# Pooled attention and a GELU layer on one core: v over 128 partitions, first batch two head pairs at a time

## The chip, the cores and the metric

The kernel runs on one core of a Trainium2 chip. The metric is the device time of an execution in microseconds (us), lower is better. The engines of the core work side by side and wait for each other on semaphores: TensorE (PE; its weight loads are listed apart as PEld), VectorE (DVE), ScalarE (ACT), GpSimd (POOL) and SyncE (SP). SP, ACT and POOL also start DMAs.

## What is computed

A batch has 8 heads, 576 rows and 64 columns a head; there are 8 batches. k and v are averaged over every 8 rows, which leaves 72 rows a head; each row of q attends to them. The result, 4608 rows of 512, goes through two matrix products with a tanh GELU between them.

```python
k_p = k.reshape(B, H, Sp, 8, D).mean(axis=3)          # v_p alike; Sp = 72
scores = scale * q @ k_p.transpose(0, 1, 3, 2)
attn = exp(scores - max); attn = attn / attn.sum(-1)
x = (attn @ v_p).transpose(0, 2, 1, 3).reshape(4608, 512)
h = x @ w_in                                          # 512 x 2048
out = gelu_tanh(h) @ w_out                            # 2048 x 512
```

## The kernel before

**Two kinds of work on one TensorE.** The attention runs by batch, 576 rows each; the two products run by group, 512 rows each, nine groups. Batch 0 is done first, alone. Then, in group g, the first product (`p1_mm`, L282: 16 tiles `fo` of 128 columns, each a sum over four slices `ko`) is followed by the second product (`p2_mm`, L291: four row tiles r, each a sum over 16 `fo`), and the attention of batch g+1 is put between the matmuls of the second product, at the positions `pos` of its 64 matmuls. Groups 7 and 8 have no attention.

**Attention of a batch.** k is loaded into 128 partitions: a main part of four rows each and a tail of 64 rows (L70, L71). v is loaded with the pooled row as partition (L79), so 72 partitions, 8 heads each. VectorE makes the pools by three additions each (L145, `k_steps`, `v_steps`). TensorE transposes pooled k (L172) and, for batches 0 and 1, q (L189); later q are transposed by a DMA that SP starts (L200). A pair of heads `pr` and a half of the rows `c` (288 of the 576) make one step of eight: scores (`qk`, L211), exponential (`expo`, L218), product with v (`av`, L231, in batch 0 L236), and the division by the sum: logarithm (L244, L245; in batch 0 L247), exponential of its negative (L249), and a multiplication on VectorE into `xT` (L257). The sums come from columns of eights that stand beside v's (in batch 0 from a tile `ones`).

**PSUM** has eight banks. Tile `fo` of a group goes to the bank that `h_bank` names, the second product's row tile to `o_bank`; VectorE copies it to `osb` (L296) and stores follow on SP (L302). The fourth tile (`fo` = 3) of a group uses the bank of the last row tile of the group before.

**The order is the program's.** There is no scheduler: each engine runs its instructions in the order in which the program issues them, and so does each DMA queue. What VectorE does beside the first product stands in `plan`: after which tile `fo` which step of the next batch comes. The products on a tile of zeros (`spin`, L312), called fillers here, put nothing to use.

**DMA order.** At the start SP loads half of k and all of v, ACT half of k and k's tail; POOL loads q, two quarters of w_in, then k and q of batch 1, two more quarters and w_out in four parts (4 MB in memory for each weight, cast to bf16 on the way). In group g, POOL loads q of batch g+2, SP transposes it by DMA, and POOL waits for that (`gate`, L358) before it loads k and v.

Of the kernel before, what the change touches and what calls it, by code (L numbers as in the profile page):

```python
# [18 lines left out]
def kernel(  # L19
# [29 lines left out]
    kvp = ctx.enter_context(tc.tile_pool(name="kvp", bufs=2))  # L49
# [12 lines left out]
    vs, qs = {}, {}  # L62
    kts = [consts.tile([128, KR + 1, 512], F32, name=f"kt{i}") for i in range(2)]

    def load_k(b, engs):
        rows = k[b].rearrange("h (j l) d -> (h j) (l d)", l=8)
        main = rows[0:128 * KR].rearrange("(p r) c -> p r c", r=KR)
        n = KR // len(engs)
        for i, eng in enumerate(engs):
            eng.dma_start(out=kts[b % 2][:, i * n:(i + 1) * n], in_=main[:, i * n:(i + 1) * n])  # L70
        engs[-1].dma_start(out=kts[b % 2][64:128, KR], in_=rows[128 * KR:])  # L71

    def load_v(b, eng, h0=0, h1=H):
        if b not in vs:
            vs[b] = kvp.tile([Sp, H, 512], F32, name="vt")
        rows = v[b, h0:h1].rearrange("h (j l) d -> j h (l d)", l=8)

        for j0, j1 in ((0, 64), (64, Sp)) if eng is nc.sync else ((0, Sp),):
            eng.dma_start(out=vs[b][j0:j1, h0:h1], in_=rows[j0:j1])  # L79
# [8 lines left out]
    w_in_b = consts.tile([128, KO, DF], BF16, name="w_in_b")  # L88
    w_out_b = consts.tile([128, FO, DM], BF16, name="w_out_b")
    w_in_v = moe_w_in.rearrange("(ko p) f -> p ko f", p=128)  # L90
    w_out_v = moe_w_out.rearrange("(fo p) d -> p fo d", p=128)
# [4 lines left out]
    load_v(0, nc.sync, 0, 4)  # L96
    load_v(0, nc.sync, 4, 8)
# [4 lines left out]
    def load_w_in(i):  # L102
        nc.gpsimd.dma_start(out=w_in_b[:, :, i * 512:(i + 1) * 512], in_=w_in_v[:, :, i * 512:(i + 1) * 512])  # L103

    load_w_in(0)
    load_w_in(1)
# [4 lines left out]
    kTs = [consts.tile([128, 2, H, Sp], BF16, name=f"kT{i}") for i in range(2)]  # L111
    kps = [consts.tile([128, KR + 2, D], BF16, name=f"kp{i}") for i in range(2)]

    vps = [consts.tile([Sp, PR, 2, 2, D], BF16, name=f"vp{i}") for i in range(2)]

    vz = consts.tile([Sp, PR, 2, 2, D], BF16, name="vz")
    ones = consts.tile([Sp, 2, 2, D], BF16, name="ones")
# [5 lines left out]
    nc.vector.memset(kTs[0], 0.0)  # L123
    nc.vector.memset(vz, 0.0)
    nc.vector.memset(ones, 0.0)
    nc.vector.memset(ones[:, 0, 0], 8.0)
    nc.vector.memset(ones[:, 1, 1], 8.0)
    nc.gpsimd.memset(kTs[1], 0.0)  # L128
    nc.gpsimd.memset(kps[1], 0.0)  # L129
    nc.gpsimd.memset(kts[1][0:64, KR], 0.0)  # L130
    nc.gpsimd.memset(vps[0], 8.0)  # L131
    nc.gpsimd.memset(vps[1], 8.0)  # L132

    load_k(1, [nc.gpsimd])
    load_q(1)
    load_w_in(2)
    load_w_in(3)
    for i in range(4):
        nc.gpsimd.dma_start(out=w_out_b[:, 4 * i:4 * i + 4, :], in_=w_out_v[:, 4 * i:4 * i + 4, :])

# [13 lines left out]
    def v_steps(b, hf):  # L154
        t = vs[b][:, hf * 4:(hf + 1) * 4]

        def s3():
            w = (vps[b % 2] if b else vz)[:, 2 * hf:2 * hf + 2]
            for e in range(2):
                add(w[:, :, e, e, :], t[:, e::2, 0:64], t[:, e::2, 64:128])  # L160

        return [lambda: add(t[:, :, 0:256], t[:, :, 0:256], t[:, :, 256:512]),
                lambda: add(t[:, :, 0:128], t[:, :, 0:128], t[:, :, 128:256]), s3]
# [4 lines left out]
    def trans_k(b, bank, odd_eng=None):  # L168
        tp = half_bank(bank)[:, 0:(KR + 1) * 128].rearrange("p (r c) -> p r c", c=128)
        kf = kps[b % 2].rearrange("p r d -> p (r d)")  # L170
        for r in range(KR + 1):
            nc.tensor.transpose(out=tp[:, r, :], in_=kf[:, r * D:r * D + 128], identity=identb)  # L172
        tp = tp[0:D]
        n7 = (H - 1) * KH
        for e in range(2):
            copy = nc.scalar.copy if e and odd_eng is nc.scalar else nc.vector.tensor_copy
            o = kTs[b % 2][e * 64:(e + 1) * 64, e]
            copy(out=o[:, 0:H - 1].rearrange("p h (j r) -> p h j r", r=KR),  # L178
                 in_=tp[:, 0:KR, 0:n7].rearrange("p r (h j) -> p h j r", j=KH))
            copy(out=o[:, H - 1, 0:(128 - n7) * KR].rearrange("p (j r) -> p j r", r=KR),  # L180
                 in_=tp[:, 0:KR, n7:128].rearrange("p r j -> p j r"))
            copy(out=o[:, H - 1, (128 - n7) * KR:], in_=tp[:, KR, 64:128])

    def trans_q(b, i, t0, n, bank, eng):
        if b not in qTs:
            qTs[b] = bp.tile([128, 2, TP, 128], BF16, name="qT")
        tp = half_bank(bank)[:, 0:n * 128].rearrange("p (t c) -> p t c", c=128)
        for x in range(n):
            nc.tensor.transpose(out=half_bank(bank)[:, x * 128:(x + 1) * 128],  # L189
                                in_=qs[b][:, i, (t0 + x) * 128:(t0 + x + 1) * 128],  # L190
                                identity=identb)
        o = qTs[b][:, i, t0:t0 + n]
        if eng is nc.scalar:
            nc.scalar.copy(out=o, in_=tp)
        else:
            nc.vector.tensor_copy(out=o, in_=tp)

# [9 lines left out]

    def qk(b, c, pr, bank):
        for e in range(2):
            h = 2 * pr + e  # L210
            nc.tensor.matmul(out=PS[:Sp, bank + e, :CH].rearrange("j (t p) -> j t p", p=32),  # L211
                             lhsT=kTs[b % 2][:, c, h, :],
# [3 lines left out]
    def expo(b, c, pr, bank):  # L216
        e = ep.tile([Sp, 2, CH], BF16, name="e", bufs=8)
        nc.scalar.activation(out=e, in_=PS[:Sp, bank:bank + 2, :CH], func=ACT.Exp, scale=1.0 / 64.0)  # L218
        es[b, c, pr] = e

    def flat(w):
        return w.rearrange("j a d -> j (a d)")

    def av(b, c, pr, bank):
# [3 lines left out]
        e = es.pop((b, c, pr))  # L228
        for x in range(2):
            if b:  # L230
                nc.tensor.matmul(out=PS[:, bank + x, :CH], lhsT=flat(vps[b % 2][:, pr, x]),  # L231
                                 rhs=e[:, x, :], start=True, stop=True)
            else:
                for y in range(2):
                    w = vz[:, pr, y] if x else ones[:, y]
                    nc.tensor.matmul(out=PS[:, bank + 1 - x, :CH], lhsT=flat(w), rhs=e[:, y, :],  # L236
# [4 lines left out]
    def norm(b, c, pr, bank):  # L241
        ld = ep.tile([128, CH], F32, name="ld")
        if b:
            nc.scalar.activation(out=ld[0:64], in_=PS[64:128, bank, :CH], func=ACT.Ln)  # L244
            nc.scalar.activation(out=ld[64:128], in_=PS[0:64, bank + 1, :CH], func=ACT.Ln)  # L245
        else:
            nc.scalar.activation(out=ld, in_=PS[:, bank + 1, :CH], func=ACT.Ln)  # L247
# [4 lines left out]
    def mult(b, c, pr, bank):  # L252
        rc = rcs.pop((b, c, pr))
        col = b * S + c * CH
        for x in range(2 if b else 1):
            rows = slice(x * 64, (x + 1) * 64) if b else slice(0, 128)
            nc.vector.tensor_tensor(out=xT[rows, pr, col:col + CH], in0=PS[rows, bank + x, :CH],  # L257
                                    in1=rc[rows], op=ALU.mult)

# [9 lines left out]
    def h_bank(g, fo):  # L269
        x, y = x_bank(g), 1 - x_bank(g)  # L270
        if fo == 4:
            return 7
# [7 lines left out]
    def p1_mm(g, fo, ko, c0=0, c1=GROUP):  # L280
        r0 = g * GROUP
        nc.tensor.matmul(out=PS[:, h_bank(g, fo), c0:c1], lhsT=w_in_b[:, ko, fo * 128:(fo + 1) * 128],  # L282
# [22 lines left out]
    act_set(EXP_SET)  # L305
    for s in k_steps(0):
        s()

    def spin(n):

        for _ in range(n):
            nc.tensor.matmul(out=PS[:, 7, :], lhsT=idle[:, 0:128], rhs=idle, start=True, stop=True)  # L312

    def scores(b, c, pr, bank):
        qk(b, c, pr, bank)
        expo(b, c, pr, bank)

    spin(16)
    trans_q(0, *QG[0], 5, nc.scalar)
    trans_q(0, *QG[1], 6, nc.scalar)  # L320
    spin(4)
    trans_k(0, 4, nc.scalar)
    trans_q(0, *QG[2], 5, nc.vector)
    trans_q(0, *QG[3], 6, nc.vector)
    spin(2)
    for i, (c, pr) in enumerate(((0, 0), (0, 1), (1, 0), (1, 1), (0, 2), (0, 3), (1, 2), (1, 3))):
        if i:
            spin(1)
        scores(0, c, pr, (2, 0)[i % 2])
    for hf in range(2):  # L330
        for s in v_steps(0, hf):
            s()

    early = [(fo, ko) for ko in range(KO) for fo in range(4)]
    take = (0, 0, 0, 0, 0, 4, 6, 6)
    for i, (c, pr) in enumerate(ORDER):
        bank = (4, 6, 0, 2, 4, 6, 4, 6)[i]
        av(0, c, pr, bank)
        norm(0, c, pr, bank)
        mult(0, c, pr, bank)  # L340
        if i == 3:

            vs[1] = kvp.tile([Sp, H, 512], F32, name="vt")
            nc.vector.memset(vs[1][:, 0, 0:1], 0.0)
            load_v(1, nc.sync)
        for fo, ko in early[:take[i]]:
            p1_mm(0, fo, ko, 0, CH)
        early = early[take[i]:]


    for g in range(NG):
        nb = g + 1 if g + 1 < B else None
        act_set(GELU_SET)
        if g + 2 < B:
# [5 lines left out]
            load_v(g + 2, nc.gpsimd)  # L360
# [3 lines left out]
        if nb is not None:  # L364
            kk = k_steps(nb)
            v0, v1 = v_steps(nb, 0), v_steps(nb, 1)
            tk = [lambda: trans_k(nb, 4)]
            if g:
                plan = {2: kk[:1], 3: kk[1:], 7: v0[:1], 8: v0[1:], 9: tk, 11: v1[:1], 12: v1[1:]}
            else:  # L370
                tq = [lambda a=a, i=i: trans_q(nb, *a, 4 + i, nc.vector) for i, a in enumerate(QG)]
                plan = {0: kk, 4: tk, 6: tq[:1], 7: tq[1:2], 8: tq[2:3], 9: tq[3:], 10: v0, 12: v1}
# [5 lines left out]
        if g == 0:  # L378
            first = [(fo, ko, CH) for ko in range(KO) for fo in range(4)]
        else:  # L380
            late = 3
            rest = [fo for fo in range(4) if fo != late]
            first = [(fo, ko, 0) for ko in range(2) for fo in rest]
            first += [(late, 0, 0), (late, 1, 0)]
            first += [(fo, ko, 0) for ko in (2, 3) for fo in rest + [late]]
        for fo, ko, c0 in first:
            p1_mm(g, fo, ko, c0)
        for fo in range(FO):
# [4 lines left out]
            for s in side[fo]:  # L393
                s()

# [6 lines left out]
        if nb is not None:  # L402
            act_set(EXP_SET)
            pos = (6, 14, 20, 27, 34, 41, 48, 55, 61)
            for i in range(len(ORDER) + 1):
# [7 lines left out]
                if i:  # L413
                    at(pos[i], norm, *a)
                    at(min(pos[i] + 9, 65), mult, *a)
# [43 lines left out]
```

The softmax here doesn't subtract the row's maximum and nothing guards it: scores larger than these inputs give would overflow.

## Time and profile before

| | |
|---|---|
| median of 8 runs | 311.26 us (310.81 to 312.35) |
| profiled execution | 311.07 us |
| its span | 309.3 us |
| granted clock | 0.998 |
| TensorE, weight loads | 297.6, 149.4 us busy |
| ScalarE, VectorE, GpSimd | 220.8, 157.1, 30.8 us busy |
| group 1, group 4 (start to next start) | 32.12, 31.85 us |
| first product of group 0 from its fifth tile | 25.85 us after the span's start |
| HBM read, written | 36.70, 9.44 MB |

The span is what the profiler sees of the execution, from its first instruction to its last; 1.8 us of the profiled execution lie around it. A product's row says how long it is in the pipeline; the next one starts earlier.

### The profile page before, as it was taken

Reading aid. Unit: us, or ns where it says so; the run is one execution under the profiler, and the core shown is the slowest. Engines: PE = TensorE matmul, PEld = TensorE weight load, DVE = VectorE, ACT = ScalarE, POOL = GpSimd, SP = SyncE. Lnnn points to the kernel's source line nnn. Section 1 sums busy time; section 2 is a strip of 40 time slices with the busy share of each in tenths; the row PEclk is TensorE's granted clock in tenths of the full one; section 3 lists DMA queues with packets and bytes.
Section 4 is the critical chain, followed back from the end, with each engine's and each line's share of the span. In section 5 each row is a group of like instructions: output and inputs, shape, how many; then the busy total and the mean of one; then the engine's idle time right before and its main releaser. Section 6 shows DMA issues by size and latency. Waiting matters only on the chain.

```text
span 309.3 us, 4278 instructions
## 1 busy us (share of the span) xinstructions
PE 297.6 (96%) x1545; PEld 149.4 (48%) x1545; DVE 157.1 (51%) x304; ACT 220.8 (71%) x414; POOL 30.8 (10%) x54
## 2 busy tenths in 40 slices
PE   6788999999999999999999999999999999999994
PEld 2455455445544455445544554455445544444441
DVE  3867536557568356855495459636772640120011
ACT  1597588877987799778987898689868986306500
POOL 8530000301201100120003000200000000000000
PEclk9999999999999999999999999999999999999999
DMA  7999996984985982598258727572101220121022
GB/s 219 238 283 247 180 202 122 271 219 80 279 214 106 245 189 52 110 242 175 69 110 240 175 70 105 168 177 67 40 0 36 51 51 2 34 68 34 2 68 69
DMA packets 32701, 41.05 MB, mean 133 GB/s; under 512 B 17608, under 2 KB 21704, under 8 KB 31784
## 3 DMA queue, kind: packets, MB, share of 16 engines
q0 software_dynamic: 10160, 24.26, 35.5%
q1 hardware_dynamic: 22200, 15.74, 21.7%
q10 hardware_dynamic: 320, 0.79, 0.9%
q8 instruction: 12, 0.20, 0.2%
q14 instruction: 9, 0.07, 0.1%
HBM read 36.70 MB, written 9.44 MB: 149 GB/s over the span
## 4 chain that ended last, share of the span: by engine, by line
PE 84%; DMA 12%; POOL 2%; issue 0%; DVE 0%; POOLq 0%
PE PS L291 39%; PE PS L282 36%; DMA w_out_b<-in_moe_w_out_dram 8%; DMA kt<-in_k_dram 4%; PE PS L231 4%; PE PS L211 4%; PE PS L172 1%; POOL w_in_b L103 0%; POOL kT L128 0%; POOL qb L84 0%; POOL vp L131 0%; POOL vp L132 0%; DVE osb L296 0%; POOL kt L130 0%; POOL kp L129 0%
## 5 line engine op out<-in xcount | busy, mean ns | idle before, releaser
L291 PE MATMUL PS<-w_out_b,gT 128*128 128x512 bf16 x576 | 136.4, 379 | 0.2 <-DMA w_out_b<-in_moe_w_out_dram 0.2
L282 PE MATMUL PS<-xT,w_in_b 128*128 128x512 bf16 (+2 forms) x592 | 129.0, 373 | 0.6 <-DMA w_in_b<-in_moe_w_in_dram 0.3
L288 ACT ACTIVATE gT<-PS 128x512 bf16<-128x512 f32 x144 | 81.2, 603 | 47.6 <-PE PS L282 47.4
L282 PEld LDWEIGHTS <-w_in_b 128*128 128x128 bf16 x592 | 57.3, 98 | 65.5 <-issue 2.0
L291 PEld LDWEIGHTS <-gT 128*128 128x128 bf16 x576 | 56.0, 97 | 57.2 <-issue 1.0
L296 DVE COPY osb<-PS 128x512 f32<-128x512 f32 x36 | 24.9, 691 | 95.4 <-PE PS L291 95.3
L257 DVE TENSOR_TENSOR xT<-PS,rc 64x288 bf16<-64x288 f32 (+1 forms) x120 | 54.5, 455 | 29.0 <-ACT rc L249 26.7
L218 ACT ACTIVATE e<-PS 72x576 bf16<-72x576 f32 x64 | 40.6, 643 | 8.6 <-PE PS L211 7.7
L145 DVE TENSOR_TENSOR vt<-vt 72x1024 f32<-72x1024 f32 (+1 forms) x32 | 30.5, 953 | 6.8 <-DMA vt<-in_v_dram 6.1
L249 ACT ACTIVATE rc<-ld 128x288 f32<-128x288 f32 x64 | 28.3, 442 | 2.0
L211 PE MATMUL PS<-qT,kT 128*72 128x288 bf16 x128 | 26.1, 286 | 0.1
L244 ACT ACTIVATE ld<-PS 64x288 f32<-64x288 f32 x56 | 22.8, 407 | 1.3
L245 ACT ACTIVATE ld<-PS 64x288 f32<-64x288 f32 x56 | 22.5, 402 | 1.3
L263 ACT ACT_TABLE_LOAD x17 | 21.8, 1283 | 2.1 <-issue 1.8
L231 PE MATMUL PS<-e,vp 72*128 72x288 bf16 x112 | 23.1, 285 | 0.0
L211 PEld LDWEIGHTS <-kT 128*72 128x72 bf16 x128 | 14.4, 113 | 14.2 <-issue 1.4
L145 DVE TENSOR_TENSOR kt<-kt 128x1280 f32<-128x1280 f32 (+1 forms) x16 | 18.5, 1158 | 5.2 <-DMA kt<-in_k_dram 4.7
L358 POOL COPY gate<-qT 1x2 bf16<-1x2 bf16 x6 | 1.0, 174 | 154.9 <-DMA qT<-qb 154.9
L178 DVE COPY kT<-PS 64x504 bf16<-64x504 bf16 x15 | 10.1, 675 | 7.2 <-PE PS L172 7.1
L231 PEld LDWEIGHTS <-vp 72*128 72x128 bf16 x112 | 11.0, 98 | 3.3
L312 PE MATMUL PS<-idle 128*128 128x512 bf16 x29 | 9.3, 436 | 1.2 <-DVE idle L120 1.2
L145 DVE TENSOR_TENSOR vp<-vt 72x128 bf16<-72x128 f32 x28 | 6.9, 284 | 0.6
(45 smaller groups left out, 75.3 us busy)
## 6 DMA issues: line engine op xcount, KB each, us to landing
out_dram<-osb SPq DMA_DIRECT2D x142, 64.0 KB, 1.7
kt<-in_k_dram POOLq DMA_DIRECT2D x7, 1024.0 KB, 5.9
vt<-in_v_dram POOLq DMA_DIRECT2D x6, 1152.0 KB, 12.7
qb<-in_q_dram POOLq DMA_DIRECT2D x7, 576.0 KB, 15.4
w_in_b<-in_moe_w_in_dram POOLq DMA_DIRECT2D x4, 512.0 KB, 17.4
w_out_b<-in_moe_w_out_dram POOLq DMA_DIRECT2D x4, 512.0 KB, 24.2
vt<-in_v_dram SPq DMA_DIRECT2D x2, 512.0 KB, 11.3
vt<-in_v_dram SPq DMA_DIRECT2D x1, 1024.0 KB, 11.5
```

What stands on the lines that cost most here:

```text
L145: nc.vector.tensor_tensor(out=o, in0=a, in1=b, op=ALU.add)
L211: nc.tensor.matmul(out=PS[:Sp, bank + e, :CH].rearrange("j (t p) -> j t p", p=32), lhsT=kTs[b % 2][:, c, h, :], rhs=qTs[b][:, h // 4, :, h ...
L218: nc.scalar.activation(out=e, in_=PS[:Sp, bank:bank + 2, :CH], func=ACT.Exp, scale=1.0 / 64.0)
L231: nc.tensor.matmul(out=PS[:, bank + x, :CH], lhsT=flat(vps[b % 2][:, pr, x]), rhs=e[:, x, :], start=True, stop=True)
L244: nc.scalar.activation(out=ld[0:64], in_=PS[64:128, bank, :CH], func=ACT.Ln)
L245: nc.scalar.activation(out=ld[64:128], in_=PS[0:64, bank + 1, :CH], func=ACT.Ln)
L249: nc.scalar.activation(out=rc, in_=ld, func=ACT.Exp, scale=-1.0)
L257: nc.vector.tensor_tensor(out=xT[rows, pr, col:col + CH], in0=PS[rows, bank + x, :CH], in1=rc[rows], op=ALU.mult)
L282: nc.tensor.matmul(out=PS[:, h_bank(g, fo), c0:c1], lhsT=w_in_b[:, ko, fo * 128:(fo + 1) * 128], rhs=xT[:, ko, r0 + c0:r0 + c1], start=(ko ...
L288: nc.scalar.activation(out=gTs[g][:, fo, :], in_=PS[:, h_bank(g, fo), :], func=ACT.Gelu_apprx_tanh)
L291: nc.tensor.matmul(out=PS[:, o_bank(g, r), :], lhsT=gTs[g][:, fo, r * 128:(r + 1) * 128], rhs=w_out_b[:, fo, :], start=(fo == 0), stop=(fo ...
L296: nc.vector.tensor_copy(out=osb, in_=PS[:, o_bank(g, r), :])
```

## The change

It has three parts and some that go with them.

- v is laid out like k: heads 0 to 3 in partitions 0 to 63, heads 4 to 7 in 64 to 127, four heads each, and the last 8 of the 72 pooled rows of all heads in a fifth column `t[:, 4]` (64 partitions). Loads are four DMAs for one or two. The last rows are pooled apart into `vl`, and two DMAs on SP put them beside the others, so that heads 0 to 3 have 72 rows and heads 4 to 7 have 128, of which 56 are zero. kT follows that order, which takes six copies for three; scores, exponential and product with v take 128 rows for heads 4 to 7.
- In batch 0, after the scores, two head pairs go together: products of both, then one logarithm, one exponential and one multiplication of 2 x 288 columns (`norm0`). The first product of group 0 is no longer split by columns; its first four tiles stand in banks 4 to 7. Fillers stand in other places and numbers (22, then one in each of six score steps, then 5, 2 and 3).
- From group 1 on, the fourth tile's first three slices come after three slices of the others; the multiplication of the step before the last comes before the last copy of outputs (62 for 64).
- w_in is loaded in two parts for four, w_out with four of its rows in one piece; the hidden columns are permuted accordingly, so that a tile's weights are every fourth column. On POOL, the second part of w_in comes before q of batch 1, and the fills of tiles after both. In group 0, q, k and v of batch 2 are asked for after the first product, and VectorE's steps come at other tiles.

```diff
-        engs[-1].dma_start(out=kts[b % 2][64:128, KR], in_=rows[128 * KR:])
+        engs[0].dma_start(out=kts[b % 2][64:128, KR], in_=rows[128 * KR:])
+    def load_v(b, engs):
+        rows = v[b].rearrange("h (j l) d -> j h (l d)", l=8)
+        t = vts[b % 2]
+        for i in range(2):
+            engs[-1].dma_start(out=t[32 * i:32 * i + 32, 4], in_=rows[64:, 4 * i:4 * i + 4])
+        for i in range(2):
+            engs[i % len(engs)].dma_start(out=t[64 * i:64 * i + 64, 0:4], in_=rows[0:64, 4 * i:4 * i + 4])
...
-    w_out_v = moe_w_out.rearrange("(fo p) d -> p fo d", p=128)
+    w_out_v = moe_w_out.rearrange("(q p j) d -> p q (j d)", p=128, j=4)
-    load_v(0, nc.sync, 0, 4)
-    load_v(0, nc.sync, 4, 8)
+    load_v(0, [nc.sync, nc.scalar])
+        nc.gpsimd.dma_start(out=w_in_b[i], in_=w_in_v[:, :, i * 1024:(i + 1) * 1024])
...
+    def v_steps(b):
+        t = vts[b % 2]
+        w = (vps[b % 2] if b else vz)[:, :, 0]
+        vl = vls[b % 2]
+        def pools(c):
+            add(t[:, c, 0:256], t[:, c, 0:256], t[:, c, 256:512])
+            add(t[:, c, 0:128], t[:, c, 0:128], t[:, c, 128:256])
+        def last():
+            add(vl, t[0:64, 4, 0:64], t[0:64, 4, 64:128])
+            for i in range(2):
+                nc.sync.dma_start(out=w[64 - 64 * i:72 - 64 * i, 4 * i:4 * i + 4], in_=vl[32 * i:32 * i + 32])
+        def main():
+            for i in range(2):
+                p = slice(64 * i, 64 * i + 64)
+                add(w[p, 4 * i:4 * i + 4], t[p, 0:4, 0:64], t[p, 0:4, 64:128])
+        return pools, last, main
...
+    def norm0(c, pr, bank):
+        ld = ep.tile([128, 2, CH], F32, name="ld0", bufs=1)
+        nc.scalar.activation(out=ld, in_=PS[:, bank + 1:bank + 4:2, :CH], func=ACT.Ln)
+        rc = ep.tile([128, 2, CH], F32, name="rc0")
+        nc.scalar.activation(out=rc, in_=ld, func=ACT.Exp, scale=-1.0)
+        nc.vector.tensor_tensor(out=xT[:, pr:pr + 2, c * CH:(c + 1) * CH], in0=PS[:, bank:bank + 3:2, :CH],
+                                in1=rc, op=ALU.mult)
-        if fo == 4:
+        if g == 0 and fo < 4:
+            return 4 + fo
+        if g and fo == 4:
             return 7
-        nc.tensor.matmul(out=PS[:, h_bank(g, fo), c0:c1], lhsT=w_in_b[:, ko, fo * 128:(fo + 1) * 128],
+        q, j = divmod(fo % 8, 4)
+        nc.tensor.matmul(out=PS[:, h_bank(g, fo), c0:c1], lhsT=w_in_b[fo // 8][:, ko, q * 512 + j:(q + 1) * 512:4],
...
-    for s in k_steps(0):
+    spin(22, 1)
+    t = kts[0]
+    for r in (slice(0, KR), slice(KR, KR + 1)):
+        add(t[:, r, 0:256], t[:, r, 0:256], t[:, r, 256:512])
+    for s in k_steps(0)[1:]:
         s()
+    load_k(1, [nc.gpsimd])
+    load_w_in(1)
+    load_q(1)
...
+    pools, last, main = v_steps(0)
+    pools(slice(4, 5))
+    last()
+    trans_k_mm(0, 4)
+    trans_k_copy(0, 0, 4, upper=False)
+    trans_k_copy(0, 1, 4, upper=False)
     trans_q(0, *QG[0], 5, nc.scalar)
     trans_q(0, *QG[1], 6, nc.scalar)
-    spin(4)
-    trans_k(0, 4, nc.scalar)
+    scores(0, 0, 2)
+    scores(0, 1, 0)
+    trans_k_copy(0, 0, 4, lower=False)
+    trans_k_copy(0, 1, 4, lower=False)
     trans_q(0, *QG[2], 5, nc.vector)
     trans_q(0, *QG[3], 6, nc.vector)
+    for i, (c, pr) in enumerate(((1, 0), (1, 1), (0, 2), (0, 3), (1, 2), (1, 3))):
+        spin(1, 7)
+        scores(c, pr, (2, 0)[i % 2])
+    pools(slice(0, 4))
+    main()
+    def av0(c, pr, bank):
+        for x in range(2):
+            av(0, c, pr + x, bank + 2 * x)
+    early = [(fo, ko) for ko in range(2) for fo in range(4)]
+    av0(0, 0, 4)
+    norm0(0, 0, 4)
+    av0(1, 0, 0)
+    norm0(1, 0, 0)
+    spin(5, 5)
+    av0(0, 2, 4)
+    norm0(0, 2, 4)
+    nc.vector.memset(vts[1][:, 0, 0:1], 0.0)
+    load_v(1, [nc.sync])
+    spin(2, 1)
+    av0(1, 2, 0)
+    norm0(1, 2, 0)
+    spin(3, 5)
+    for fo, ko in early:
+        p1_mm(0, fo, ko)
...
-                plan = {2: kk[:1], 3: kk[1:], 7: v0[:1], 8: v0[1:], 9: tk, 11: v1[:1], 12: v1[1:]}
+                plan = {2: kk[:1], 3: kk[1:], 7: [lambda: pools(slice(0, 5))], 8: [last, main], 9: tk}
-                plan = {0: kk, 4: tk, 6: tq[:1], 7: tq[1:2], 8: tq[2:3], 9: tq[3:], 10: v0, 12: v1}
+                plan = {0: kk, 6: tk, 10: tq[:1], 11: tq[1:2], 12: tq[2:3],
+                        13: tq[3:] + [lambda: pools(slice(0, 5)), last, main]}
-            first = [(fo, ko, 0) for ko in range(2) for fo in rest]
-            first += [(late, 0, 0), (late, 1, 0)]
-            first += [(fo, ko, 0) for ko in (2, 3) for fo in rest + [late]]
+            first = [(fo, ko) for ko in range(3) for fo in rest]
+            first += [(late, ko) for ko in range(3)]
+            first += [(fo, 3) for fo in rest + [late]]
+        if g == 0:
+            load_next()
-                    at(min(pos[i] + 9, 65), mult, *a)
+                    at(min(pos[i] + 9, 62 if i < len(ORDER) else 65), mult, *a)
```

## The prediction

> **What bounds the kernel now.** I read the page's busy times first, then a table of stretches cut at the groups' starts, then the order of time at those seams where a stretch is longer than its work.
>
> ```profile
> span 309.3 us, 4278 instructions
> PE 297.6 (96%) x1545; PEld 149.4 (48%) x1545; DVE 157.1 (51%) x304; ACT 220.8 (71%) x414; POOL 30.8 (10%) x54
> ```
>
> TensorE is the bound, 96% of the span. The stretches (us, length, then busy time of each engine) say where it isn't: the first 25.85 us belong to batch 0, the next 31.82 to group 0, the next ones to groups 1 to 6.
>
> ```profile
> 0.00:25.85 25.85, 19.91 (x132) 12.28 (x133) 15.92 (x34) 15.22 (x32) 14.02 (x25) 1.00 1.05 243
> 25.85:57.67 31.82, 30.33 (x169) 15.40 (x168) 17.55 (x36) 24.38 (x47) 2.93 (x5) 1.00 1.05 188
> 57.67:89.79 32.12, 32.11 (x166) 16.13 (x165) 19.35 (x37) 26.61 (x51) 2.92 (x5) 1.00 0.81 213
> 154.03:185.88 31.85, 31.85 (x166) 16.14 (x165) 19.25 (x37) 26.59 (x51) 2.90 (x5) 1.00 0.61 145
> ```
>
> A clean group takes 31.85 us; groups 1 to 3 take 32.12. Every product of 512 columns starts 0.216 us after the one before it (64 in 13.81 us in the chain), though its row says 379 ns; so behind each printed wait of TensorE 0.16 us more are lost. Groups 7 and 8 run without a gap. What can move is the first 58 us and 0.27 us in each of three groups. In order of time, TensorE, ScalarE and VectorE (start, length, idle before):
>
> ```profile
> 7.30 2.35 DVE L145 TENSOR_TENSOR kt<-kt 128x1280 f32<-128x1280 f32 x2 [3.87 <-DMA kt<-in_k_dram]
> 13.10 1.18 ACT L218 ACTIVATE e<-PS 72x576 bf16<-72x576 f32 x2 [0.51 <-PE PS L211]
> 17.60 0.40 ACT L247 ACTIVATE ld<-PS 128x288 f32<-128x288 f32 x1
> 24.45 0.46 DVE L257 TENSOR_TENSOR xT<-PS,rc 128x288 bf16<-128x288 f32 x1 [0.85 <-ACT rc L249]
> 27.84 0.44 PE L172 MATMUL PS<-identb,kp 128*128 128x128 bf16 x5 [0.96 <-DVE kp L145]
> 35.84 3.63 PE L282 MATMUL PS<-xT,w_in_b 128*128 128x512 bf16 x16 [0.28 <-DMA w_in_b<-in_moe_w_in_dram]
> 46.07 0.81 PE L291 MATMUL PS<-w_out_b,gT 128*128 128x512 bf16 x3 [0.17 <-DMA w_out_b<-in_moe_w_out_dram]
> 57.67 4.53 PE L282 MATMUL PS<-xT,w_in_b 128*128 128x512 bf16 x19
> ```
>
> Batch 0 is a chain: load of k, adds, exponentials from 13.10, first logarithm at 17.60, last multiplication at 24.91; ScalarE has no rest in it. 26 products from 23.58 (six of 288 columns, 16 of 224, four of 512) put the fifth tile of group 0 at 25.85. Group 0 then loses 1.12 us to the adds of k, 0.44 to w_in, 0.33 to w_out, and 0.23 where 0.07 is left before the first transpose of q: 2.12.
>
> [...] The trace has no strided load[...]. [...] Here the first fillers start 0.43 us apart and from 4.1 us on 0.216. [...] the stores here land 1.7 us after issue.
>
> **The change, part by part.**
>
> *Start.* The first add of k no longer waits for k's tail: SP's half is issued at 0.75 and lands 5.8 later, so VectorE starts at 6.6, not 7.30. Adds of 1.22 (as 72x1024), 0.42 (its slope), 0.83 and 0.49 end at 9.7 (before: 10.18). v's last pools and half of kT's copies go behind them: 0.42 + 0.29 + 0.22 and two of 0.45, to 11.6. TensorE transposes k at 9.9 and q, now behind k in its queue, from 10.25; ScalarE's two copies of q begin 0.5 later and take 1.18, to 11.9; the scores take 0.06 and the first exponential follows 0.44 later, at 12.4 (before: 13.10). Eight took 4.6; I add 0.1 for the second half of q, now ahead of the third: ScalarE is free at 17.1. Meanwhile VectorE makes ten small copies of kT (1.4), two of q (0.91), and v's adds of 1.22 + 0.69 + 0.42, ready at 16.3; v has landed, on two queues, before 14 (16.6 before, on one). Eight products of v take 0.98 from 16.3, and the first logarithm starts 0.33 after the last of them started: 17.5, against 17.60.
>
> *Two pairs at a time.* The program's order shows what each filler waits for: the five for the first multiplication, the two for the second, the three for the third. So they lie in the chain. For 576 columns I take 0.65 (logarithm, near the exponential of scores, 0.643), 0.69 (0.442 + 0.25) and 0.755 (0.455 + 288 at 1.04 ns); with hand-overs 2.15 from logarithm to end of multiplication. From 17.5: first multiplication ends 19.65; five fillers 1.08; eight products 0.98; third logarithm at 21.98, 4.48 after the first; third multiplication ends at 24.13; three fillers 0.65 to 24.84; 16 products of 512 columns 3.45: the fifth tile starts at 28.3. The fourth multiplication ends at 25.5, under them. ScalarE does less (4 x 1.34 against 8 x 0.78), but no pair waits for ScalarE alone now. Against 25.85: **+2.45**.
>
> *Group 0.* k of batch 1 is added from 25.5 to 28.3, hidden under the tiles, as its transposes come two tiles later, at 31: 1.12 gone. w_in as two loads of 4 KB rows and w_out in 8 KB rows move the same bytes in half and a quarter of the pieces; w_in was just 0.28 late and is needed 2.5 us later; w_out's first quarter by 40. I take both waits, and that of q (its transposes come at fo 10), as gone: **-2.12**. If the larger rows bring nothing, w_out still lands as before, under a product that starts 0.7 later: at most 0.3 back. What is late next is v's last pools. Their DMA waits on SP for VectorE, whose adds of v follow the fourth copy of q: p1 ends at 28.3 + 11.66 = 39.96 (before: 13.45 less 1.79 of waits), that copy at 39.1, adds 1.49 + 0.83 + 0.22, so issue at 41.7 and landing, 1.7 as for a store, at 43.4. The products of v come 3.27 into the second product, at 43.2: **+0.2** (0.1 to 1.0 for landings of 1.6 to 2.5). Behind them in TensorE's queue stands all else.
>
> *Groups 1 to 3.* Tile 3 waited for the copy of the last outputs (57.87 to 58.56) and xT's third slice for the multiplication behind it. Now the slice's multiplication stands before the copy, its factor ready at 57.41: slice at 58.4 for a use at 58.97, copy done 59.1 for a use at 59.61, fourth slice at 60.0 for 60.26. **3 x -0.27 = -0.81**.
>
> *Hidden in every group.* Twelve kT copies for six add some 0.8 us to VectorE, v's adds over 128 partitions take off 1.6 (4.9 to 3.3): VectorE is busy 19 of 32. v comes in four loads for one, 1.8 us more issue on an idle GpSimd. The two small DMAs stand on SP behind the transposing DMA of q: in group 1 that started at 71.2, 13.5 us in; behind it they'd land at 75.6 for a use at 75.1, 0.5 late. q waits behind w_out, k and v, which end sooner, so I take nothing. Weight loads overlap products of 0.216: 98 ns could double unseen.
>
> Sum: 2.45 - 2.12 + 0.2 - 0.81 = **-0.28**, span 309.0. The profiled execution took 311.07 with a span of 309.3, the median is 311.26: I predict 311.0.
>
> **Rivals.**
> *Fillers are free.* If TensorE's fillers and waits cover time that ScalarE needs anyway, the start stays at 25.85 and the sum is -2.73: 308.5; with half of it, 309.8. For it: ScalarE's work in this stretch shrinks by 0.9. Against: each filler's wait.
> *Half clock (slower).* Between the end of the fillers (22: some 7.4) and the first scores (12.0) stand only 14 transposes, 0.8 us in 4.6; before, 9 in the 3.35 between two runs of fillers, and the clock held. If it falls, a filler and two scores take 0.92 a round, above ScalarE's 0.575: 0.35 in each of some four rounds, 1.4 in all, 312.4. [...]
> *Small DMAs late.* 1 us in group 0 and 0.5 in group 1 more: 312.5.
> *Strided weight loads show.* They count from 216 ns; at 250, 576 x 0.034 = 20 us: 331. Doubled, nothing.
>
> **How the numbers follow.** A measurement of this kernel tells 0.2%, 0.6 us, from no change. The sum as worked, 310.4 to 311.7, has a chance of 0.46 (0.13 of it faster, 0.27 same, 0.06 slower). Free fillers, in whole or in half: 0.26, faster. Half clock 0.16, late DMAs 0.08, strided loads 0.02: slower, 0.26. The last 0.02 are same. Faster 0.39, same 0.29, slower 0.32. The range leaves out the lower half of free fillers and strided loads: 308.8 to 312.7.
>
> **What would show it.** First exponential near 12.4, first logarithm near 17.5, fifth tile of group 0 near 28.3; fillers waiting for the multiplications; no wait of TensorE for k, w_in, w_out in group 0 and one of some 0.2 for v's small DMA; groups 1 to 3 at 31.85; weight loads under 216 ns. Wrong it would be by a fifth tile before 27 or after 29.5, by products 0.43 us apart after 10 us, or by a waiting of SP that reaches the products of v.

## The result, and the profile after

The changed kernel takes 314.01 us (median) against 311.40: a ratio of 1.0086, 95% interval 1.0073 to 1.0100. The forecast was 311.0, at most 312.7. The profiled execution took 312.47 with a span of 310.7, which is 1.4 more than before; it was the only one of twelve whose granted clock was 1.0. The eleven others had 0.988 to 0.995 and took 313.5 to 315.9. So there are two losses to find: 1.4 us that this profile shows, and some 1.5 that it doesn't.

The head of the page, and the stretches cut at the groups' starts (first batch 0, then group 0, group 1, group 4; length, then busy time of TensorE, its weight loads, VectorE, ScalarE, GpSimd):

```profile
span 310.7 us, 4365 instructions
...
PE 299.2 (96%) x1538; PEld 157.1 (51%) x1538; DVE 150.4 (48%) x333; ACT 219.6 (71%) x403; POOL 41.0 (13%) x76
```

```profile
0.00:28.28 28.28, 22.96 (x126) 12.18 (x126) 18.75 (x44) 14.23 (x21) 15.24 (x29) 1.00 1.01 253
28.28:59.96 31.68, 29.79 (x168) 16.05 (x167) 15.01 (x38) 24.02 (x47) 4.41 (x8) 1.00 0.85 207
59.96:91.81 31.85, 31.85 (x167) 17.01 (x166) 18.15 (x41) 26.63 (x51) 4.42 (x8) 1.00 0.86 187
155.51:187.36 31.85, 31.85 (x167) 17.01 (x166) 18.14 (x41) 26.63 (x51) 4.41 (x8) 1.00 0.60 145
```

The start is 2.43 us longer (28.28 for 25.85) and groups 1 to 3 are clean at 31.85, both as forecast. Group 0 should have shrunk by about 1.9 and shrank by 0.14. The order of time shows where it lost that:

```profile
11.66 1.85 ACT L248 ACTIVATE e<-PS 72x576 bf16<-72x576 f32 x3 [0.49 <-PE PS L240]
17.46 0.65 ACT L294 ACTIVATE ld<-PS 128x576 f32<-128x576 f32 x1 [0.98 <-PE PS L269]
19.67 1.24 PE L351 MATMUL PS<-idle 128*128 128x512 bf16 x5 [1.26 <-DVE xT L297]
24.83 5.34 PE L325 MATMUL PS<-xT,w_in_b 128*128 128x512 bf16 x24
30.87 0.44 PE L175 MATMUL PS<-identb,kp 128*128 128x128 bf16 x5
40.87 2.35 DVE L137 TENSOR_TENSOR vt<-vt 128x1280 f32<-128x1280 f32 x2 [1.98 <-DMA vt<-in_v_dram]
43.53 1.56 SPq L159 DMA_DIRECT2D vp<-vl  x2
45.48 0.41 PE L264 MATMUL PS<-e,vp 72*128 72x288 bf16 x2 [1.88 <-DMA vp<-vl]
```

No wait for k, w_in or w_out is left. Instead TensorE stands 2.04 us (1.88 printed and the 0.16 that every such wait hides) for v's small DMA, where 0.2 was forecast. VectorE waited for v until 40.87, and the DMA issued at 43.53 let TensorE go at 45.48; by the semaphore events of the trace it landed at 45.3, 1.8 us after its issue. The account closes: 2.43 - 2.18 (group 0's waits of before, by e10 below) + 2.04 - 0.81 = 1.48, for 1.4 measured.

### The profile page after: what moved, and what is told of

The parts are those of the page before. It is cut to its first block, busy times and chain, and to the rows that moved or that the text cites. A ratio compares the mean times of both kernels' runs of the same rounds, so it can differ in the third digit from the quotient of the medians.

```text
span 310.7 us, 4365 instructions
## 1 busy us (share of the span) xinstructions
PE 299.2 (96%) x1538; PEld 157.1 (51%) x1538; DVE 150.4 (48%) x333; ACT 219.6 (71%) x403; POOL 41.0 (13%) x76
## 4 chain that ended last, share of the span: by engine, by line
PE 85%; DMA 9%; DVE 2%; ACT 1%; ACTq 1%; issue 1%; SPq 0%; DVEq 0%
PE PS L334 39%; PE PS L325 36%; DMA vt<-in_v_dram 9%; PE PS L264 5%; PE PS L240 4%; DVE vt L137 1%; ACTq L79 1%; PE PS L269 1%; DMA vp<-vl 1%; PE PS L175 1%; ACT rc L296 0%; ACT ld L294 0%; PE PS L351 0%; DVE xT L297 0%; DVE osb L339 0%
## 5 line engine op out<-in xcount | busy, mean ns | idle before, releaser
L325 PE MATMUL PS<-xT,w_in_b 128*128 128x512 bf16 x576 | 127.6, 379 | 0.0
L288 DVE TENSOR_TENSOR xT<-PS,rc 64x288 bf16<-64x288 f32 x112 | 51.0, 455 | 32.6 <-ACT rc L280 30.3
L248 ACT ACTIVATE e<-PS 72x576 bf16<-72x576 f32 (+1 forms) x64 | 40.9, 646 | 8.7 <-PE PS L240 7.8
L240 PE MATMUL PS<-qT,kT 128*72 128x288 bf16 (+1 forms) x128 | 26.0, 286 | 1.3 <-ACT qT L215 1.0
L264 PE MATMUL PS<-e,vp 72*128 72x288 bf16 (+1 forms) x112 | 23.1, 286 | 1.9 <-DMA vp<-vl 1.9
L240 PEld LDWEIGHTS <-kT 128*72 128x72 bf16 (+1 forms) x128 | 13.4, 105 | 15.5 <-DVE kT L185 1.0
L137 DVE TENSOR_TENSOR vt<-vt 128x1280 f32<-128x1280 f32 (+5 forms) x18 | 18.8, 1044 | 3.1 <-DMA vt<-in_v_dram 2.8
L137 DVE TENSOR_TENSOR kt<-kt 128x640 f32<-128x640 f32 (+3 forms) x17 | 18.7, 1099 | 1.9 <-DMA kt<-in_k_dram 1.4
L185 DVE COPY kT<-PS 64x288 bf16<-64x288 bf16 (+2 forms) x48 | 13.0, 319 | 6.3 <-PE PS L175 6.1
L264 PEld LDWEIGHTS <-vp 72*128 72x128 bf16 (+1 forms) x112 | 10.9, 98 | 5.9 <-issue 2.1
```

The costliest lines, as they stand in the source:

```text
L137: nc.vector.tensor_tensor(out=o, in0=a, in1=b, op=ALU.add)
L240: nc.tensor.matmul(out=PS[:n, bank + e, :CH].rearrange("j (t p) -> j t p", p=32), lhsT=kTs[b % 2][c][:, h, :n], rhs=qTs[b][:, h // 4, :, h ...
L248: nc.scalar.activation(out=e[:n], in_=PS[:n, bank:bank + 2, :CH], func=ACT.Exp, scale=1.0 / 64.0)
L264: nc.tensor.matmul(out=PS[:, bank + x, :CH], lhsT=window(vps[b % 2][:n], 2 * pr + x), rhs=e[:n, x, :], start=True, stop=True)
```

## The experiments

Theories for the 1.4 us: *late load* (v of batch 1, let go behind the third multiplication at 24.1, lands at 40.7, and all behind it is late), or *backlog* (the DMA engines are full until about 45, and a small DMA lands when what they hold has landed, whenever it is issued). For the 1.5 us that the profile doesn't show: *half clock*, or something in the loads. For the +2.43 at the start: *chain* (fillers wait for multiplications) or *free fillers*. Unless said otherwise the short diffs are against the changed kernel. Every ratio is to the kernel before, and "full clock" means a granted clock of 0.998 or more.

**Half clock: fillers at 10 us.**

```diff
     trans_q(0, *QG[1], 6, nc.scalar)
+    spin(5, 7)
     scores(0, 0, 2)
```

> The changed kernel with five more fillers, behind the transposes of q and ahead of the first scores, where TensorE stood from 10.0 to 11.2 us. Half clock: if the time that the unprofiled executions took beyond the profiled one (314.0 against 312.5) is [...] set off by the empty stretch after the first fillers, the granted clock goes from 0.995 back to 0.998 or more in most executions and the time falls by 1.5 us, to 312.5. Rival, the fillers do nothing and the 1.5 us come from elsewhere (later in the program, or from the loads): clock 0.995 and 314.0 as before. The late load of v stays in both.

312.67 us, ratio 1.0057 (1.0038 to 1.0077). In ten of fourteen executions the clock was 0.998 or more, median 312.5; the other four had a median of 314.2. So the 1.5 us go with the clock, not with the loads. The traces of e8 and e9 below each hold a stretch of 3.4 us at half rate; by an estimate from them, one such stretch makes a clock of 0.9945 over 312 us. Eight of the changed kernel's eleven had 0.994 or 0.995.

**Late load: v let go sooner.**

```diff
     norm0(0, 0, 4)
+    nc.vector.memset(vts[1][:, 0, 0:1], 0.0)
+    load_v(1, [nc.sync])
     av0(1, 0, 0)
...
-    nc.vector.memset(vts[1][:, 0, 0:1], 0.0)
-    load_v(1, [nc.sync])
```

> The changed kernel with the one edit that v of batch 1 is let go behind the first multiplication of batch 0 (19.6 us) and not behind the third (24.1). Late load: if the wait of 1.88 us for v's small DMA in group 0 comes from v landing at 40.7, v lands some 4 us sooner, the adds begin behind the fourth copy of q at 38.9, the small DMA lands at 43.4 and the wait is 0 to 0.3: 1.6 to 1.9 us faster, 312.2. Rival, crowded queues: the loads of k, w_in and w_out of that stretch share the same DMA engines, v lands hardly sooner or something else lands later, and at most 0.5 us is won. The half clock, if there is one, stays.

312.30 us, ratio 1.0020 (1.0009 to 1.0032), but not for the reason given. The order of time of this kernel:

```profile
38.74 2.34 DVE L137 TENSOR_TENSOR vt<-vt 128x1280 f32<-128x1280 f32 x2
...
41.40 1.57 SPq L159 DMA_DIRECT2D vp<-vl  x2
...
45.39 0.41 PE L264 MATMUL PS<-e,vp 72*128 72x288 bf16 x2 [1.86 <-DMA vp<-vl]
```

v is there and its adds start 2.1 sooner, the DMA is issued 2.1 sooner, and TensorE still waits 1.86 us and goes on at 45.39. Late load has fallen as the whole cause: with v in time, the landing is held at 45.2 by something else. At full clock this kernel is no faster (312.3 against 312.47). What it gained in the median is the cost of the half clock: its sixteen executions below 0.998 take 312.3 too. That fits a landing that doesn't depend on TensorE any more, so that a later start only eats into the wait; no profile of such an execution was kept.

**The small DMA ten tiles earlier.**

```diff
-   13: tq[3:] + [lambda: pools(slice(0, 5)), last, main]}
+   7: [lambda: pools(slice(4, 5)), last], 13: tq[3:] + [lambda: pools(slice(0, 4)), main]}
```

> The changed kernel with the adds of v's last pools and their two small DMAs ten tiles earlier in group 0 (behind the transposes of k at tile 7), the adds of the other four rows left where they are. Late load: the wait for the small DMA goes from 1.88 to 0, and the other rows, landed at 40.7 and added in 2.3 us, are ready at 43.2 to 43.4: at most 0.2 of wait is left, 1.7 us faster, 312.3. Rival, the wait is the small DMA's own slowness (issue and landing, 1.8 us, whatever it waits behind): it goes too, and only the e2 kernel, in which the small DMA stays in its place, tells them apart. Rival, v's main rows were the wait all along: under 0.5 us faster.

311.38 us, ratio 0.9984 (0.9970 to 0.9998): no slower than the kernel before. No wait for the small DMA is left. Issued at 35.9, the first still needed 6.9 us to land, by the semaphore events of the trace. The four executions at full clock took 310.3, 2.1 less than the changed kernel's one: the term of group 0, and a little more.

**Backlog: q of batch 2 behind v's adds.** With `e2` and without it:

```diff
         if g == 0:
+            nc.gpsimd.tensor_copy(out=gate, in_=vls[1][0:1, 0:2])
             load_next()
```

> The e2 kernel with one more edit: the load of q of batch 2 (0.59 MB, behind w_out in GpSimd's queue) is let go only when v's last pools of batch 1 are added (41.1 us), and not as soon as the queue reaches it. Backlog: if the small DMA of e2, issued at 41.4 and landed at 45.2, waited on the DMA engines behind the packets of that load, it now lands by 43.2 and TensorE's wait of 1.86 us falls to 0.2 or less; the profiled span at full clock goes from 310.6 to 308.9. Late load of v, or a DMA that is slow in itself: the wait stays at 1.5 us or more, 310.6. Rival, q of batch 2 is now late itself: a wait in front of the scores of group 1 takes the place.

> The changed kernel with the load of q of batch 2 behind v's adds, v of batch 1 let go where the changed kernel has it. Backlog: v's main rows share the DMA engines with one load fewer and land at 37 to 39 and not at 40.7; the adds begin behind the fourth copy of q or soon after, at 38.8 to 39.2, the small DMA is issued at 41.7 and lands by 43.4: wait 0.2, span 309.0 at full clock. If the loads ahead of q's in the queue hold v back, it lands at 40.7 still and the small DMA at 45.2: span 310.7.

With the earlier v (e5) the small DMA, issued at 42.81, lands at 44.6: 1.8 us later, for 3.8 in e2, and the first wait is gone; q's load now stands in front of the second small DMA:

```profile
42.81 1.57 SPq L159 DMA_DIRECT2D vp<-vl  x2
...
44.54 0.41 PE L240 MATMUL PS<-qT,kT 128*72 128x288 bf16 x2
44.78 0.41 PE L264 MATMUL PS<-e,vp 72*128 72x288 bf16 x2
...
48.33 0.41 PE L240 MATMUL PS<-qT,kT 128*128 128x288 bf16 x2
49.41 0.40 PE L264 MATMUL PS<-e,vp 128*128 128x288 bf16 x2 [0.67 <-DMA vp<-vl]
```

This profile lost clock early (0.992) and has all of this 1.4 us later than e2. Moved back by that, the landing is at 43.2 and TensorE comes at 43.4, so by this estimate the wait is gone at full clock too. Backlog is shown for the kernel with v in time: with one load out of the way the landing came 2 us sooner, and 0.8 us (0.67 printed) came back in front of the second. e5 takes 312.60 in all (1.0023, 1.0012 to 1.0034), since this kernel lost clock in nearly all executions; the one at 1.0 took 311.38, one us less than the changed kernel's. The other (e8), with v let go at 25.8, missed: 315.06 us, 1.0120 (1.0096 to 1.0143). v landed 16.5 us after it was let go, as in the changed kernel (16.6), so q's load isn't what holds it. The small DMA was issued late and landed 1.8 us after that; TensorE stood 1.94 us for it. So taking q away gains nothing while v is late, as v in time (e2) gains nothing while q is there. The profile of e8 also holds the half rate of which the changed kernel's shows nothing, with the program the same up to there:

```profile
19.72 1.91 PE L351 MATMUL PS<-idle 128*128 128x512 bf16 x5 [1.26 <-DVE xT L297]
21.43 0.69 PE L269 MATMUL PS<-e,ones 128*128 128x288 bf16 x2
21.91 0.69 PE L269 MATMUL PS<-e,vz 128*128 128x288 bf16 x2
...
45.10 1.57 SPq L159 DMA_DIRECT2D vp<-vl  x2
47.05 0.41 PE L264 MATMUL PS<-e,vp 72*128 72x288 bf16 x2 [1.78 <-DMA vp<-vl]
```

Products of 288 columns stand 0.240 apart here, 0.122 before 19 us and after 23.5; e3 and e5 have the same from 19.6 to 22.4. In these three profiles the half rate begins at the wait for the first multiplication (1.26 us printed in each).

**q behind the second small DMA** (against e5):

```diff
-            nc.gpsimd.tensor_copy(out=gate, in_=vls[1][0:1, 0:2])
+            nc.gpsimd.tensor_copy(out=gate, in_=vps[1][0:1, H // 2, 0, 0:2])
```

> The e5 kernel with the load of q of batch 2 let go behind the second of the two small DMAs of v, not behind the adds. In e5 TensorE waits 0.84 us more for the second one, issued 0.8 behind the first and landed at 49.3, together with q's. If that one waited behind q's packets, the wait goes: 0.8 us faster than e5 in executions of the same clock (full clock 310.6 for 311.4). If q of batch 2 comes too late by it, a new wait shows in group 1 and nothing is gained.

A miss by its second branch: 312.87 us, 1.0045 (1.0026 to 1.0065), 311.75 at full clock. Group 0 has no wait for v left, but q of batch 3 is transposed late as well, and group 1's small DMA stands behind that on SP:

```profile
11.06 1.12 PE L240 MATMUL PS<-qT,kT 128*72 128x288 bf16 x4 [1.04 <-ACT qT L215]
...
77.85 0.42 PE L264 MATMUL PS<-e,vp 72*128 72x288 bf16 x2 [1.47 <-DMA vp<-vl]
```

The first line, four products of 288 columns in 1.12 us where the changed kernel takes 0.65, is the half clock in a second place: from 11.1 to 14.4, between the first fillers and the scores.

**Chain: the same fillers on other banks.**

```diff
-    spin(5, 5)
+    spin(5, 7)
...
-    spin(2, 1)
+    spin(2, 3)
...
-    spin(3, 5)
+    spin(3, 7)
```

> The changed kernel with the same 5, 2 and 3 fillers, written to the banks that the logarithms leave (7, 3 and 7) and not to 5, 1 and 5, so that they wait for the first, second and third logarithm and not for the multiplications. Chain: the fillers go out of the chain of batch 0; third logarithm 20.9 for 21.98, fifth tile of group 0 at 26.6 for 28.28, and the empty 1.26 us before the first multiplication is filled, so that the granted clock is 1.0 more often. Backlog: the small DMA of v lands at 43.5 to 45 all the same, so the wait in front of v's products grows to 3 us or more and the span hardly moves (310.3 to 310.7, median 312.2). If the late load of v were the whole cause, v would be let go 1.1 sooner and the span fall by 1.1 to 309.6. Rival, fillers are free already: fifth tile at 28.3, nothing gained.

314.01 us, 1.0075 (1.0050 to 1.0101). The fillers now wait for a logarithm and not for the multiplication behind it:

```profile
22.98 6.20 PE L325 MATMUL PS<-xT,w_in_b 128*128 128x512 bf16 x28 [0.23 <-DVE vt L412]
...
45.41 0.64 PE L264 MATMUL PS<-e,vp 72*128 72x288 bf16 x2 [3.66 <-DMA vp<-vl]
45.84 2.77 PE L334 MATMUL PS<-w_out_b,gT 128*128 128x512 bf16 x6
```

The first product starts 1.85 sooner and the fifth tile at 26.43: so much of the +2.43 was the fillers' waiting, and free fillers has fallen. All of it is given back in front of v's products, which start at 45.41 as ever. Behind that wait six products take 2.77 us instead of 1.46: half rate, by the starts of the products from 45.4 to 51.5, in this profile (clock 0.989) and, by a clock of 0.988 or 0.989, in four others. The one execution at 0.999 took 312.42.

**More fillers in the empty stretch, the chain kept.**

```diff
+    spin(6, 7)
     spin(5, 5)
```

> The changed kernel with six more fillers ahead of the five, on bank 7, which the first logarithm leaves at 18.1 us: they fill the 1.26 us in which TensorE waits for the first multiplication and leave the chain as it is. The profiles of e3, e5 and e8 show products at half rate from 19.6 to 22.4 or 23.5, behind this empty stretch. If the stretch sets it off, the granted clock is 0.998 or more in most executions and the time 312.5 (1.5 us faster), fifth tile at 28.3. If the empty stretch at 10 to 11.2, which e1 filled, is what counts, clock 0.995 and 314.0 stay.

313.32 us, 1.0065 (1.0042 to 1.0087): half a hit at most. Four of ten executions had 0.998 or more and took 312.6; so few don't tell it from the changed kernel's one of twelve, while ten of fourteen with e1's fillers do. The profile is one at 0.994; it keeps full rate from 18 to 25 and loses it here:

```profile
45.88 0.41 PE L264 MATMUL PS<-e,vp 72*128 72x288 bf16 x2 [2.10 <-DMA vp<-vl]
46.12 2.48 PE L334 MATMUL PS<-w_out_b,gT 128*128 128x512 bf16 x6
```

So the half rate also begins behind the wait for the small DMA (at 46.4, by the starts of the products). Which of the three places shows it differs between the profiles; of the changed kernel's own none tells it.

**One part alone.** On the kernel before, only the order of the fourth tile and the multiplication ahead of the copy:

```diff
-    first = [(fo, ko, 0) for ko in range(2) for fo in rest]
-    first += [(late, 0, 0), (late, 1, 0)]
-    first += [(fo, ko, 0) for ko in (2, 3) for fo in rest + [late]]
+    first = [(fo, ko, 0) for ko in range(3) for fo in rest]
+    first += [(late, ko, 0) for ko in range(3)]
+    first += [(fo, 3, 0) for fo in rest + [late]]
...
-    at(min(pos[i] + 9, 65), mult, *a)
+    at(min(pos[i] + 9, 62 if i < len(ORDER) else 65), mult, *a)
```

> The kernel before with one part of the change alone: in groups 1 to 8 the fourth tile's products over three slices behind the other tiles', and the multiplication ahead of the copy of the last outputs. As forecast: 0.27 us in each of three groups, 0.8 us faster, 310.6. Rival, the part brings nothing without the rest (the waits in groups 1 to 3 only move): 311.4.

310.84 us, ratio 0.9983 (0.9974 to 0.9992): 0.5 us, with 0.8 inside the interval. Its groups 1 to 3 take 31.85 each.

**Together.** e7 is the edits of e1, e5 and e6 in one kernel; e10 has, on top, those of e11 and e3:

```diff
-            nc.gpsimd.tensor_copy(out=gate, in_=vls[1][0:1, 0:2])
+            nc.gpsimd.tensor_copy(out=gate, in_=vps[1][0:1, H // 2, 0, 0:2])
...
-   13: tq[3:] + [lambda: pools(slice(0, 5)), last, main]}
+   7: [lambda: pools(slice(4, 5)), last], 13: tq[3:] + [lambda: pools(slice(0, 4)), main]}
```

> The edits of e1 (five fillers behind the transposes of q), e5 (v of batch 1 let go behind the first multiplication, q of batch 2 behind v's adds) and e6 (fillers on the banks of the logarithms) together. Chain and backlog as stated: fifth tile at 26.6, no wait for v's small DMA above 0.5, full clock in most executions: span 307.2, time 309.0, faster than both kernels. If the DMA engines are behind by more than q's load, v's small DMA lands at 43 against a need at 41.7: 308.5 and 310.3.

> The e7 kernel with q of batch 2 behind the second small DMA, and v's last pools with their small DMAs at tile 7 of group 0 as in e3. Backlog: the two waits of e7 for the small DMAs (0.43 and 0.33) go, span 307.0, 308.9 us. If the early small DMA, issued near 32, stands behind w_out's packets until 42 all the same, it lands no sooner than in e7: 0.3 of gain at most, 309.3.

309.63 us, 0.9936 (0.9920 to 0.9953), and 308.77 us, 0.9916 (0.9894 to 0.9938), with a clock of 0.998 or more in every execution. The first still waits for both small DMAs:

```profile
42.14 0.41 PE L264 MATMUL PS<-e,vp 72*128 72x288 bf16 x2 [0.27 <-DMA vp<-vl]
...
46.27 0.41 PE L264 MATMUL PS<-e,vp 128*128 128x288 bf16 x2 [0.17 <-DMA vp<-vl]
```

Its first landed at 42.0, just behind the last of w_out. In the second they were issued from 33.2 and landed by 40.4, and nothing waits. Its two first stretches:

```profile
0.00:26.83 26.83, 23.17 (x129) 12.43 (x132) 18.15 (x43) 14.25 (x21) 14.54 (x28) 1.00 1.00 260
26.83:56.47 29.64, 29.46 (x166) 16.11 (x168) 15.93 (x41) 23.86 (x47) 4.95 (x10) 1.00 0.87 184
```

Group 0 takes 29.64 us for 31.82 before, so the 2.12 us of the forecast are there to be had (2.18). The changed kernel's own 31.68, less its wait of 2.04, is 29.64 as well. With +0.98 at the start and -0.81 in groups 1 to 3 the span falls by 2.0; it fell from 309.3 to 307.2.

**Rows of w_out and the stride** (against e7):

```diff
-    w_out_v = moe_w_out.rearrange("(q p j) d -> p q (j d)", p=128, j=4)
+    w_out_v = moe_w_out.rearrange("(fo p) d -> p fo d", p=128)
...
-        q, j = divmod(fo % 8, 4)
-        nc.tensor.matmul(out=PS[:, h_bank(g, fo), c0:c1], lhsT=w_in_b[fo // 8][:, ko, q * 512 + j:(q + 1) * 512:4],
+        nc.tensor.matmul(out=PS[:, h_bank(g, fo), c0:c1], lhsT=w_in_b[fo // 8][:, ko, fo % 8 * 128:fo % 8 * 128 + 128],
...
-        nc.gpsimd.dma_start(out=w_out_b[:, 4 * i:4 * i + 4, :].rearrange("p j d -> p (j d)"), in_=w_out_v[:, i])
+        nc.gpsimd.dma_start(out=w_out_b[:, 4 * i:4 * i + 4, :], in_=w_out_v[:, 4 * i:4 * i + 4, :])
```

> The e7 kernel with w_out in rows of 1 KB as before, and w_in's weights taken in adjacent columns, so that weight loads have no stride (w_in still in two loads of rows of 4 KB). If strided weight loads stay hidden and larger rows bring nothing, 309.6 as e7, weight loads back from 113 to 98 ns. If the rows of w_out matter to the backlog, w_out and v land later and the wait for v's small DMA grows by 0.5 us or more: 310.2 or above. If the stride costs TensorE anything, faster than e7 by over 0.3.

310.02 us, 0.9955 (0.9937 to 0.9974). The weight loads of w_in, of the changed kernel and of this one:

```profile
L325 PEld LDWEIGHTS <-w_in_b x576: 112/113/117, 24.6 to 292.0; 128*128 128x128 bf16 x192
```

```profile
L324 PEld LDWEIGHTS <-w_in_b x576: 95/98/98, 23.0 to 289.7; 128*128 128x128 bf16 x192
```

The stride costs 15 ns a load and no time: products stay 0.216 apart in both. What the rows are worth is not shown. The medians differ by 0.39 us, from ten and five executions that overlap (309.4 to 310.6, 309.4 to 310.0). In this profile the first wait for v's small DMA is 0.97 for 0.43, but the second (0.33) is gone, and the first product starts 0.47 later, behind adds of k that began 0.67 later (6.76 for 6.09). With 1 KB rows w_out lands whole at 42.8, hardly outside the 41.5 to 42.8 of the eleven profiles with 8 KB rows. One figure stands out: the second half of v's main rows took 12.2 us from issue to landing, for 14.0 to 14.8 in the five profiles with 8 KB rows and v let go at the same place (e2, e5, e7, e10, e11). So the larger rows of w_out may have slowed v's load beside them. No run has the changed kernel with 1 KB rows.

## Why the prediction was wrong

*Start, +2.45:* right, +2.43. First logarithm 17.46 (17.5), third 21.98 (21.98), fifth tile 28.28 (28.3). The first exponential came 0.7 sooner than worked out (11.66), which changed nothing, as v's adds set the logarithm. The rival that fillers are free fell with e6.

*Group 0, -2.12:* right; e10 shows -2.18 with the new wait gone.

*v's small DMA, +0.2 (0.1 to 1.0):* this step failed; it measured 2.04. The sum let VectorE's adds of v follow the fourth copy of q and put the landing of v itself at nothing. That copy ended at 38.9 (39.1), but v landed at 40.7: VectorE stood 1.98 us, the small DMA was issued at 43.53 for 41.7 and landed at 45.3 for 43.4. Its own 1.8 us from issue to landing were near the 1.7 of the forecast. When v was let go and when its adds began, before and after:

```profile
21.33 1.16 SPq L79 DMA_DIRECT2D vt<-in_v_dram  x2
35.63 1.94 DVE L145 TENSOR_TENSOR vt<-vt 72x1024 f32<-72x1024 f32 x2 [1.27 <-DMA vt<-in_v_dram]
```

```profile
24.18 1.33 SPq L81 DMA_DIRECT2D vt<-in_v_dram  x2
40.87 2.35 DVE L137 TENSOR_TENSOR vt<-vt 128x1280 f32<-128x1280 f32 x2 [1.98 <-DMA vt<-in_v_dram]
```

v was let go 2.85 later, as its release stands behind the third multiplication, which the prediction had at 24.13 without carrying it on to v. By itself this would put the landing at 38.5, in time. But v also took 16.6 us for 14.3. What slowed it stays open: it isn't q (16.5 in e8), and e12 points at the rows of w_out.

A second error lay behind the first. Issued at 41.4 (e2), close to the forecast's 41.7, the small DMA needed 3.8 us and not 1.7. The price of 1.7 nearly holds where the DMA engines have little to do: 1.8 in the changed kernel, with their busy share at 0.17 in the half us behind the issue and 0.05 or less from 44.0 to 45.3, and 1.8 in e5, ahead of q's load. But the page of before had the DMA engines at or near full in this stretch. The two lines are their busy tenths from 18 to 50 us, in 40 slices of 0.8, before and after:

```profile
DMA  9999999999999999999999999999999999974100
```

```profile
DMA  9999999999999999999999999999997410029993
```

Full until 46 before and about 43 after, with q of batch 2 landing whole only at 44.7: the small DMA of e2, issued into this at 41.4 (the engines nine tenths busy), landed at 45.2. So two limits ended at the same time, near 45.3. Repairing v alone gained nothing in the profile (e2), nor did taking q's load away (e8); both together took the first wait away (e5), and an earlier issue gets round both (e3, e10). By the semaphore events of e2's trace the shares of the small DMA landed from 43.8 to 45.25, in step with the last shares of q (43.6 to 45.05) and about 0.2 us behind them. By what rule the engines held it behind q no run shows.

*Groups 1 to 3, -0.81:* right (31.85 each; e4).

*Half clock, a rival at 0.16:* it happened, in the eleven executions below 0.998, and cost 1.5 us. That 1.4 had been worked out is in part luck: the sum was for the scores, and where the changed kernel lost its 1.5 no profile shows. The place named, ahead of the first scores, is one of three, and e1, which filled it, is the edit after which the clock clearly came back. But in the profile that holds the half clock there (e11) it delayed the fillers behind the first multiplication by only 0.62 (20.29 for 19.67); at the wait for the first multiplication it delayed the first product by 1.3 (26.13 in e3, for 24.83). That wait and the one for v's small DMA are the other two places. I read only the stretch that the change had emptied of fillers and not the waits that it created. The kernel before loses clock too, with less than 0.998 in 73 of 120 executions: 311.7 against 310.9 at 0.998 or more, so it pays 0.7 where the change pays 1.5.

*The range:* small DMAs late and half clock were weighed as separate cases, 0.08 and 0.16, and both came. They are linked in part: in e6 and e9 the half rate begins at the wait for the small DMA. But e3, which has no such wait, had the full clock in only four of fourteen executions. With 1.84 more for the wait, and 1.0 for the half clock (1.5, less the 0.5 by which the median before, 311.4, lies above its 310.9 at full clock), 311.0 becomes 313.8, near the 314.0 measured. Both terms are measured ones, so this closes the account and tests nothing.

*Strided loads:* 113 ns (98 adjacent, e12), below 216; nothing, as forecast.

## What to carry to other kernels

When a change moves the release of a load, carry that on to its landing and to all that waits for it. Price a small DMA by what the DMA engines hold when it is issued (here 3.8 us behind q's load, in e2), not by its latency on nearly idle ones (1.8): find the last big load in flight and ask whether that one could go behind. When a repair does what it should and gains nothing, look for a second limit that ends at the same time, and try both repairs together. Give fillers a buffer that comes free early; the same ten fillers cost 1.85 us more in the chain on banks that the multiplications read than on ones that the logarithms leave. A wait on TensorE can cost twice: 3.4 us at half rate began at one of 1.26 us in e8 and behind one of 2.10 in e9, so count its length and the clock that may fall behind it.

## What the runs showed of the hardware

A stretch at half rate lasted 3.4 us in two profiles (20.1 to 23.5 in e8, 46.4 to 49.8 in e9). The longest empty stretch ahead of it was 1.4 us in e8 (1.26 printed and 0.16) and 2.3 in e9 (2.10 and 0.16), with work on both sides. Five fillers in an empty stretch brought a clock of 0.998 or more in ten of fourteen executions (e1), for one of twelve without them; how long an empty stretch must be to lower the clock no run shows. The first fillers ran at half rate (0.43 us apart) until 4.1 us in the profile before and until 7.1 in the one after. A DMA of 4 KB (the first small one of v) needed 1.8 us from issue to landing ahead of q (e5, e8) and with the DMA engines at a busy share of 0.17 and less (the changed kernel), 3.8 behind q (e2), 6.0 behind w_out and the end of v (e10), and 6.9 behind w_out, v and q (e3).
